# A banded attention and SOLU kernel with all its steps in a new order, w_in loaded from ScalarE, masks made on VectorE and a shorter rebuild of the sinks' values

## The chip, the cores and the metric

The kernel runs on one core of a Trainium2 chip, as one launch. The metric is the device time of the program in microseconds (us). Times of 531.01, 531.22 and 532.69 us were measured before the change; their median is 531.22 us. TensorE is called PE below, VectorE DVE, ScalarE ACT, GpSimd POOL and SyncE SP, as the profile calls them.

## The reference

Attention with a window and a few sink positions, and then a two-layer block with a normalisation between its matrix products, are computed in float32:

```python
B, H, S, D = 4, 8, 768, 64          # n_sink 4, window 128
scores = q @ k.T / sqrt(D)
keep   = (key < n_sink) | (0 <= query - key < window)
a      = softmax(where(keep, scores, -1e9))
x      = (a @ v) laid out as [B * S, H * D]          # 3072 tokens of 512
h      = x @ w_in                                    # 512 x 1024, float64 in memory
solu   = h * softmax(h)
ln     = (solu - mean) / sqrt(var + 1e-6) * g_ln
out    = ln @ w_out                                  # 1024 x 512, float64 in memory
```

The result is 3072 x 512 float32. The weights arrive as 64-bit numbers, so that the kernel has to turn their bits into float32 itself.

## The kernel before, in words

The 3072 tokens are cut into 24 chunks of 128 queries, six for each of the four batches. With a window of 128, a chunk of queries needs only its own 128 keys, the 128 before them, and the sink positions. The first chunk of a batch (chunks 0, 6, 12 and 18, "batch-first" below) has no keys before it, and so neither the second half of its scores nor the products with old values.

Float32 products are made out of pieces. Every operand is split into a high part in a type that PE multiplies fast (fp32r) and the rest, and a product is the sum of two or three such matmuls. So each chunk needs, beside its arithmetic, casts on ACT (`k_hi`, `q_hi`, `v_hi`, `x_hi`, `u_hi`, `p_hi`), subtractions for the rests on POOL (`k_lo`, `q_lo`, `v_lo`, `x_lo`) or DVE (`p_lo`, `u_lo`), and transposes on PE (`turn_q`, `turn_k`, `turn_p`, `turn_u`, `turn_sinks`), which write tiles qt, kt, ptp, utp and skp.

A chunk goes through these stages: loads of q, k and v; transposes of q and k; `score` (PE, tile s, one per head, in two PSUM buffers that the transposes of q and k share); `pick` and `mask` (DVE) which choose the half of a score tile and add the bias; `exps` (ACT); `invert` and `normalise` (DVE); transposes of the probabilities; `part_new` and `part_old` (POOL), which cut them into the new and the old half; `value` (PE, tile av); `gather` (DVE); `shift` (a copy by DMA) and `tokens` (POOL); `hidden` (PE, L611, 24 matmuls into tile h); `highest` and `peak` (DVE, L618 and L623), `solu_exp`, `solu`, `centre`, `square`, `variance` and `root`; `turn_u`; `project` (PE, L680, 24 matmuls into tile o); `scale` (ACT, L685) and `store`. The instruction of `peak`, one per chunk, is used below as the mark of a chunk's progress.

The weights come in 16 blocks of 128 x 512, eight of w_in and eight of w_out. Each block goes through `fetch_w` (a load of 512 KB from SP's queue), `size_w` (ACT, L304), `least_w`, `move_w`, `sign_w` and `rest_w` (four instructions on DVE, L311, L315, L319 and L324), for w_out `gain_w` (ACT), then `w_hi` (ACT) and `w_lo` (POOL, or DVE for four blocks). The raw words lie in buffers that later stages use too.

Two more pieces matter here. `masks` builds the biases and selectors once, from n_sink and window, which `fetch_small` loads into tile words and `scalars` turns into tile val; all of it runs on POOL (L244 to L281). `sink_values` builds, once per batch, a tile vsink out of the eight sink rows of v: on DVE seven instructions (L403, L404, L407 and L408 twice, L411).

The order of all the work is written out by hand. The table `PLAN` holds for each stage a place relative to its chunk, `PLAN_W` holds a place for each piece of weight work, and every step is sorted by `16 * n + place`, with n the chunk. Each engine then works through its own instructions in the sequence that results, and an instruction that waits holds up everything behind it on its engine. All DMAs are issued from SP's queue, in that queue's order.

## Time and profile before

| what | value |
|---|---|
| median of three runs | 531.22 us |
| the profiled execution's own time | 529.93 us |
| its span, first to last instruction | 528.2 us |
| PE busy | 466.8 us (88%), 2756 matmuls |
| DVE, ACT, POOL busy | 411.6, 373.7 and 377.1 us |
| mean granted PE clock | 0.988 |
| DMA, mean over the span | 101 GB/s |

The span is what the trace sees. The execution's own time is 1.7 us longer, and the median of the runs is another 1.3 us above that. Matmuls are pipelined, and the length shown for one (about 400 ns for 512 columns) is about twice the distance between the starts of two; so the starts are what to read. A busy share is an average over a beginning, a long middle and an end which have different limits.

### The profile page before, as it was taken

The page shows a single profiled execution, that of the slowest core. Times are in us where ns is not written, and L with a number is a line of the kernel's source. Part 1 is how long each engine was busy: PE and PEld are TensorE (multiplying, and loading weights), DVE is VectorE, ACT ScalarE, POOL GpSimd, SP SyncE. Part 2 cuts the span into 40 slices and gives each one's busy share as a digit, 9 for nine tenths or more (in the row PEclk, how much of TensorE's full clock was granted, in tenths as well). Part 3 has the DMA queues.
Part 4 walks back from the last instruction along what each step waited for, and adds up shares of the span by engine and source line. Part 5 has one row for each costly group of instructions (what it writes and reads, how often), then busy time and mean ns, then how long its engine had stood idle before and what let it go on. Part 6 is the DMA issues. An engine that isn't in the chain of part 4 may idle for free. (4 is left out here: it accounts for less than half of the span.)

```text
span 528.2 us, 9656 instructions
## 1 busy us (share of the span) xinstructions
PE 466.8 (88%) x2756; PEld 401.9 (76%) x2756; DVE 411.6 (78%) x1199; ACT 373.7 (71%) x1034; POOL 377.1 (71%) x511
## 2 busy tenths in 40 slices
PE   0054688999997999999997999999997999999995
PEld 0044567888886888888886888888886888888883
DVE  4999999987878777788688687787678778878531
ACT  3487587887785787787675688687776778766442
POOL 3969398997885387887874587778766688777520
PEclk9999998999999899999998999999999999999999
DMA  7768244333442333443532343443343344210101
GB/s 269 225 177 218 74 107 101 90 101 94 100 104 77 91 101 92 104 110 86 124 91 74 92 114 83 108 95 101 89 102 90 91 103 108 75 55 21 33 30 46
DMA packets 104203, 53.41 MB, mean 101 GB/s; under 512 B 80528, under 2 KB 92816, under 8 KB 104144
## 3 DMA queue, kind: packets, MB, share of 16 engines
q1 hardware_dynamic: 104144, 52.72, 38.6%
q8 instruction: 25, 0.41, 0.3%
q14 instruction: 34, 0.28, 0.2%
HBM read 27.53 MB, written 6.42 MB: 64 GB/s over the span
## 5 line engine op out<-in xcount | busy, mean ns | idle before, releaser
L611 PE MATMUL h<-w1h,xh 128*128 128x512 f32 x192 | 87.4, 455 | 0.0
L680 PE MATMUL o<-w2h,uh 128*128 128x512 f32 x192 | 77.9, 406 | 0.2 <-ACT uh L669 0.2
L461 PE MATMUL s<-ring,qT 128*128 128x264 f32 (+1 forms) x192 | 58.2, 312 | 22.1 <-DVE nmx L479 20.8
L611 PE MATMUL h<-w1l,xh 128*128 128x512 f32 x192 | 77.4, 403 | 0.2 <-DVE w1l L340 0.2
L611 PE MATMUL h<-w1h,xl 128*128 128x512 f32 x192 | 77.2, 402 | 0.0
L489 ACT ACTIVATE sc<-sc,nmx 128x136 f32<-128x136 f32 (+1 forms) x192 | 76.4, 405 | 0.0
L680 PE MATMUL o<-w2l,uh 128*128 128x512 f32 x192 | 75.8, 395 | 0.2 <-DVE z L641 0.2
L680 PE MATMUL o<-w2h,ul 128*128 128x512 f32 x192 | 75.8, 395 | 0.0
L578 DVE TENSOR_REDUCE y<-av 128x256 f32<-128x512 f32 x96 | 65.4, 683 | 4.9 <-PE av L572 3.4
L600 POOL TENSOR_TENSOR xl<-xt,xh 128x256 fp32r<-128x256 f32 x48 | 35.8, 745 | 39.1 <-ACT xh L596 34.2
L461 PEld LDWEIGHTS s<-ring,qT 128*128 128x128 f32 x192 | 38.6, 201 | 31.0 <-issue 19.8
L479 DVE CUSTOM_DVE_ANT_0 sc<-s,bias 128x136 f32<-128x136 f32 (+1 forms) x192 | 51.3, 292 | 13.3 <-PE s L462 10.1
L522 POOL TENSOR_SCALAR_AFFINE_SELECT pc<-pt 128x1024 fp32r<-128x1024 f32 x40 | 44.8, 1121 | 21.7 <-DVE pt L515 21.7
L462 PE MATMUL s<-ring,qX 128*128 128x264 f32 (+1 forms) x192 | 55.9, 300 | 0.1
L393 POOL TENSOR_TENSOR vs<-vn,vs 128x256 fp32r<-128x256 f32 x48 | 36.7, 765 | 20.7 <-ACT vs L388 20.7
L419 PE MATMUL qt<-ident_r,qs 128*128 128x128 f32 x192 | 23.9, 251 | 30.9 <-POOL qs L371 29.1
L500 DVE TENSOR_TENSOR sc<-sc,rs 128x544 f32<-128x544 f32 (+1 forms) x48 | 50.7, 1057 | 0.0
L591 POOL TENSOR_TENSOR xt<-y,ysh 64x256 f32<-64x256 f32 x48 | 35.9, 748 | 16.6 <-DMA ysh<-y 9.4
L528 POOL TENSOR_SCALAR_AFFINE_SELECT pt<-pt 128x1024 fp32r<-128x1024 f32 x40 | 46.6, 1166 | 1.5
L618 DVE TENSOR_REDUCE mx<-h 128x1 f32<-128x512 f32 x48 | 30.9, 686 | 21.5 <-PE h L611 21.3
L468 DVE COPY_PREDICATED s<-m_cur,s 128x128 f32<-128x128 int32 x96 | 26.5, 291 | 25.2 <-PE s L462 25.1
L419 PEld LDWEIGHTS qt<-ident_r,qs 128*128 128x128 f32 x192 | 20.9, 146 | 32.0 <-POOL qs L371 30.5
(123 smaller groups left out, 1451.2 us busy)
## 6 DMA issues: line engine op xcount, KB each, us to landing
qX<-qT SPq DMA_DIRECT2D x96, 128.0 KB, 2.3
...
```

What stands on the lines that cost most here:

```text
L393: nc.gpsimd.tensor_tensor(vs[:, :, 1:3, :], st["vn", n][:, hb * HB:(hb + 1) * HB, :].rearrange("p (r x) d -> p r x d", x=2), vs[:, :, 0:4: ...
L419: nc.tensor.transpose(tr[:, j, :], sp[:, j, :, :].rearrange("p t d -> p (t d)"), ident_r)
L461: nc.tensor.matmul(o, st["qT", n, hb][:, j, :], rhs, start=True, stop=False)
L462: nc.tensor.matmul(o, st["qX", n, hb][:, j, :], rhs, start=False, stop=True)
L479: nc.vector.tensor_tensor_reduce(out=st["sc", n, hb][:, j, c0:c1], in0=st["s", n, h].rearrange("p a x -> p (a x)")[:, c0:c1], in1=bias0 if ...
L489: nc.scalar.activation(sc[:, i, c0:c1], sc[:, i, c0:c1], AF.Exp, bias=nmx[:, i:i + 1], scale=-1.0, accum_out=ssum[:, i:i + 1])
L500: nc.vector.tensor_tensor(sc[:, :, c0:c1], sc[:, :, c0:c1], rs.unsqueeze(2).to_broadcast([P, HB, c1 - c0]), op=ALU.mult)
L522: nc.gpsimd.affine_select(pc, pt.bitcast(F32), pattern=[[0, HB * 2], [1, P]], compare_op=ALU.is_ge, fill=0.0, base=0, channel_multiplier=-1)
L528: nc.gpsimd.affine_select(pt, pt.bitcast(F32), pattern=[[0, HB * 2], [-1, P]], compare_op=ALU.is_ge, fill=0.0, base=-1, channel_multiplier=1)
L578: nc.vector.tensor_reduce(st["y", n, hb][:, jp], st["acc", n, pr].rearrange("p x s q -> p x q s"), axis=AX.X, op=ALU.add)
L611: nc.tensor.matmul(st["h", n][:, cols], a[:, kt % 2, :], w[:, kt, cols], start=(kt == 0 and m == 0), stop=(kt == KT1 - 1 and m == 2))
L680: nc.tensor.matmul(st["o", n], a[:, kt % 4, :], w[:, kt, :], start=(kt == 0 and m == 0), stop=(kt == KT2 - 1 and m == 2))
```

## The change

Five things change.

- The order: `PLAN` and `PLAN_W` get new numbers. A table `FIRST` adds an offset for the batch-first chunks. A table `OWN` gives the chunks 0, 1, 2, 3, 22 and 23 places of their own, one per step.
- The eight blocks of w_in are loaded from ACT's queue, in place of SP's, into eight buffers of their own. Those buffers are later taken by the two parts of w_out, which are now four pairs of tiles where two large ones were.
- `masks` for the biases and `barred` run on DVE, as 14 instructions, where they ran on POOL as 15; the selectors for `pick` stay on POOL.
- `sink_values` uses two instructions on ACT and three on DVE, where it used seven on DVE.
- One more small tile (`sign`) is made on POOL.

```diff
--- before.py
+++ after.py
-    "load_k": (-51.2,),
-    "load_q": (-59.1,),
...
+    "load_k": (-50.0,),
+    "load_q": (-60.35,),
...
+FIRST = {
+    "load_k": -19.1, "load_q": -20.67, "load_v": -0.71, "k_hi": -5.17, "k_lo": -2.74, "q_hi": -3.98, "q_lo": 2.77,
...
+OWN = {
+    0: (-2861.7, -2852.81, -679.14, -1022.07, -613.22, -636.58, -560.9, -1019.84, -1022.34, -648.21, -648.23,
...
+W2P = 4
...
-    wts = [consts.tile([P, r // P, m], F32R, name=nm)
-           for nm, r, m in (("w1h", DM, DFF), ("w1l", DM, DFF), ("w2h", DFF, DM), ("w2l", DFF, DM))]
+
+    wpool = ctx.enter_context(tc.tile_pool(name="wpool", bufs=2 * W2P))
+    wts = [consts.tile([P, DM // P, DFF], F32R, name=nm) for nm in ("w1h", "w1l")] + [[None] * W2P, [None] * W2P]
...
     def barred(out, keep):
-        nc.gpsimd.tensor_scalar(out, keep, 0.5, -NEG, op0=ALU.is_lt, op1=ALU.mult)
+        nc.vector.tensor_scalar(out, keep, 0.5, -NEG, op0=ALU.is_lt, op1=ALU.mult)
...
     def masks(_, j):
         if j == 0:
 
-            nc.gpsimd.tensor_scalar(near, rel, w_f, None, op0=ALU.is_lt)
-            at_least(near, near, 1)
-            nc.gpsimd.tensor_scalar(old, ki, n_f, None, op0=ALU.is_lt)
-            nc.gpsimd.tensor_copy(is_sink.rearrange("p g s -> p (g s)"), old[:, 0:NSK])
-            nc.gpsimd.tensor_tensor(old, old, near, op=ALU.add)
+            nc.vector.tensor_scalar(near, rel, 0.0, None, op0=ALU.is_ge)
+            nc.vector.scalar_tensor_tensor(near, rel, w_f, near, op0=ALU.is_lt, op1=ALU.mult)
+            nc.vector.scalar_tensor_tensor(old, ki, n_f, near, op0=ALU.is_lt, op1=ALU.max)
             barred(bias0, old)
         elif j == 1:
 
-            nc.gpsimd.tensor_scalar(old, rel, float(P), w_f, op0=ALU.add, op1=ALU.is_lt)
-            at_least(old, old, -1)
-            nc.gpsimd.tensor_tensor(old, old, near, op=ALU.add)
+            nc.vector.tensor_scalar(is_sink.rearrange("p g s -> p (g s)"), ki[:, 0:NSK], n_f, None, op0=ALU.is_lt)
+            nc.vector.tensor_scalar(old, rel, float(P), w_f, op0=ALU.add, op1=ALU.is_lt)
+            nc.vector.scalar_tensor_tensor(old, rel, 0.0, old, op0=ALU.is_lt, op1=ALU.mult)
+            nc.vector.tensor_tensor(old, old, near, op=ALU.max)
             barred(bias1[:, 4:SEG], old)
-            nc.gpsimd.tensor_scalar(far.rearrange("p g s -> p (g s)"), rel[:, 0:NSK], float(P), w_f,
+            barred(bias2[:, 4:SEG], old)
+            nc.vector.tensor_scalar(far.rearrange("p g s -> p (g s)"), rel[:, 0:NSK], float(P), w_f,
                                     op0=ALU.add, op1=ALU.is_ge)
-            nc.gpsimd.tensor_tensor(far, far, is_sink, op=ALU.mult)
-            nc.gpsimd.tensor_copy(bias2[:, 4:SEG], bias1[:, 4:SEG])
+            nc.vector.tensor_tensor(far, far, is_sink, op=ALU.mult)
...
+            nc.gpsimd.tensor_tensor(sign, even, odd, op=ALU.subtract)
...
+    def part(w, kt, cols=slice(None)):
+        return w[kt // 2][:, kt % 2, cols] if isinstance(w, list) else w[:, kt, cols]
+
     raws = {}
     three = [("u", 2), ("u", 2), ("e", 1)]
-    raw_tags = three + [("pt", 3)] * 3 + [("pc", 2)] * 2 + three * 3
 
     def fetch_w(_, j):
         _, _, src, kt, cols = blocks[j]
-        tag, bufs = raw_tags[j]
-        raws[j] = sb.tile([P, NB, 2], I32, tag=tag, name=f"wraw_{j}", bufs=bufs)
-        nc.sync.dma_start(raws[j].rearrange("p f w -> p (f w)"), src.bitcast(I32)[kt * P:(kt + 1) * P,
-                                                                                 2 * cols.start:2 * cols.stop])
+        if j < NW1:
+            raws[j] = wpool.tile([P, NB, 2], I32, tag="w2", name=f"wraw_{j}")
+        else:
+            tag, bufs = three[j % 3]
+            raws[j] = sb.tile([P, NB, 2], I32, tag=tag, name=f"wraw_{j}", bufs=bufs)
+
+        queue = nc.scalar if j < NW1 else nc.sync
+        queue.dma_start(raws[j].rearrange("p f w -> p (f w)"), src.bitcast(I32)[kt * P:(kt + 1) * P,
+                                                                               2 * cols.start:2 * cols.stop])
...
     def w_hi(_, j):
-        wh, _, _, kt, cols = blocks[j]
-        nc.scalar.copy(wh[:, kt, cols], st["w", j])
+        wh, wl, _, kt, cols = blocks[j]
+        if j >= NW1 and wh[kt // 2] is None:
+            for nm, w in (("w2h", wh), ("w2l", wl)):
+                w[kt // 2] = wpool.tile([P, 2, DM], F32R, tag="w2", name=f"{nm}_{kt // 2}")
+        nc.scalar.copy(part(wh, kt, cols), st["w", j])
...
             raw = st["vsraw", b]
-            four = sb.tile([P, 8, D], F32R, tag="ob", name=f"vsx_{b}", bufs=2)
-            hi, lo, tmp = four[:, 0, :], four[:, 1, :], four[:, 2:4, :].bitcast(F32)
-            nc.vector.tensor_copy(hi, raw)
-            nc.vector.tensor_tensor(lo, raw, hi.bitcast(F32), op=ALU.subtract)
+            four = sb.tile([P, 8, D], F32, tag="ob", name=f"vsx_{b}", bufs=2)
+            raw_odd, tmp = four[:, 0, :], four[:, 1:3, :]
+
             vk = sb.tile([P, NPAIR, 2 * D], F32R, tag="vsink", name=f"vsink_{b}", bufs=1)
-            for i, (x, y) in enumerate(((hi, lo), (lo, hi))):
-                nc.vector.tensor_scalar(tmp[:, i, :], y.bitcast(F32), odd, None, op0=ALU.mult)
-                nc.vector.scalar_tensor_tensor(tmp[:, i, :], x.bitcast(F32), even, tmp[:, i, :],
-                                               op0=ALU.mult, op1=ALU.add)
+            nc.scalar.copy(vk[:, 0, 0:D], raw)
+            nc.scalar.activation(raw_odd, raw, AF.Copy, scale=odd)
+            nc.vector.scalar_tensor_tensor(tmp[:, 0, :], vk[:, 0, 0:D].bitcast(F32), sign, raw_odd,
+                                           op0=ALU.mult, op1=ALU.add)
+            nc.vector.tensor_tensor(tmp[:, 1, :], raw, tmp[:, 0, :], op=ALU.subtract)
 
             nc.vector.tensor_tensor(vk, tmp.rearrange("p t d -> p (t d)").unsqueeze(1).to_broadcast([P, NPAIR, 2 * D]),
                                     mine.to_broadcast([P, NPAIR, 2 * D]), op=ALU.mult)
...
-    steps = [(16 * n + at, o, n, i, f) for o, f in enumerate(stages) for n in range(NCH)
-             for i, at in enumerate(PLAN[f.__name__])]
+    index = {(name, i): j for j, (name, i) in enumerate((name, i) for name in PLAN for i in range(len(PLAN[name])))}
+
+    def when(n, name, i):
+        if n in OWN:
+            return OWN[n][index[name, i]]
+        return round(16 * n + PLAN[name][i] + (FIRST.get(name, 0) if n % NC == 0 else 0), 2)
+
+    steps = [(when(n, f.__name__, i), o, n, i, f) for o, f in enumerate(stages) for n in range(NCH)
+             for i in range(len(PLAN[f.__name__]))]
```

The tables say little by themselves. What they do to the engines' rows is shown at three places. The names in the rows carry the chunk, then a running number.

The first place is DVE at the beginning of the second batch (chunk 6 is batch-first; the tiles of chunk 7 are what DVE works on there). vsx and vsink are the tiles of `sink_values`, s_7_5 the scores of chunk 7 and head 5. Before:

```order
L403 CAST vsx_1_2139<-vsraw_1_1494 128x64
L404 TENSOR_TENSOR vsx_1_2139<-vsraw_1_1494,vsx_1_2139 128x64
L407 TENSOR_SCALAR vsx_1_2139<-vsx_1_2139,odd_110 128x64
L408 SCALAR_TENSOR_TENSOR vsx_1_2139<-vsx_1_2139,even_109 128x64
L407 TENSOR_SCALAR vsx_1_2139<-vsx_1_2139,odd_110 128x64
L408 SCALAR_TENSOR_TENSOR vsx_1_2139<-vsx_1_2139,even_109 128x64
L411 TENSOR_TENSOR vsink_1_2142<-vsx_1_2139,mine_112 128x512
L468 COPY_PREDICATED s_7_5_2148<-m_cur_105,s_7_5_2148 128x128
L479 ISA sc_7_1_2164,nmx_7_1_2165<-s_7_5_2148,bias1_103 128x136
L479 ISA nmx_7_1_2165 128x1
L515 TENSOR_TENSOR pt_6_1_2155<-ptp_6_1_2111,pt_6_1_2155 128x4x128
L468 COPY_PREDICATED s_7_4_2168<-m_cur_105,s_7_4_2168 128x128
```

Now:

```order
L663 TENSOR_REDUCE y_6_0_2150<-av_6_0_2181 128x256
L553 COPY_PREDICATED s_7_7_2201<-m_cur_106,s_7_7_2201 128x128
L564 ISA sc_7_1_2098,nmx_7_1_2099<-s_7_7_2201,bias1_104 128x136
L564 ISA nmx_7_1_2099 128x1
L600 TENSOR_TENSOR pt_6_1_2165<-ptp_6_1_2107,pt_6_1_2165 128x4x128
L492 SCALAR_TENSOR_TENSOR vsx_1_2226<-vsink_1_2227,sign_112,vsx_1_2226 128x64
L494 TENSOR_TENSOR vsx_1_2226<-vsraw_1_1612,vsx_1_2226 128x64
L496 TENSOR_TENSOR vsink_1_2227<-vsx_1_2226,mine_114 128x512
L585 TENSOR_TENSOR sc_7_0_1992<-sc_7_0_1992,rs_7_0_2184 128x544
L758 TENSOR_TENSOR ul_4_0_2264<-utp_4_0_2194,uh_4_0_2254 128x512
L579 TENSOR_SCALAR rs_7_1_2266<-ssum_7_1_2100 128x4
```

The seven instructions stood between the scores of head 3 and those of heads 4 to 7; the three that are left stand behind the last score of chunk 7.

The second place is PE in a middle chunk. qt, kt, utp and ptp are transposes; h and av are matmuls. Before:

```order
L419 MATMUL qt_12_0_3379<-ident_r_91,qs_12_0_3226 128x128 x4
L461 MATMUL s_11_7_3384<-ring_115,qT_11_1_3181 128x264
L462 MATMUL s_11_7_3384<-ring_115,qX_11_1_3223 128x264
L665 MATMUL utp_8_1_3387<-ident_86,u_8_3261 128x128 x2
L611 MATMUL h_9_3287<-w1h_59,xh_9_0_3243 128x512
L611 MATMUL h_9_3287<-w1l_60,xh_9_0_3243 128x512
L611 MATMUL h_9_3287<-w1h_59,xl_9_0_3285 128x512
L665 MATMUL utp_8_1_3387<-ident_86,u_8_3261 128x128 x2
L611 MATMUL h_9_3287<-w1h_59,xh_9_1_3353 128x512
L611 MATMUL h_9_3287<-w1l_60,xh_9_1_3353 128x512
L611 MATMUL h_9_3287<-w1h_59,xl_9_1_3355 128x512
```

Now, around the same transposes of chunk 8 (utp_8_1):

```order
L504 MATMUL qt_12_1_3436<-ident_r_92,qs_12_1_3214 128x128 x4
L696 MATMUL h_9_3332<-w1h_62,xh_9_1_3371 128x512
L696 MATMUL h_9_3332<-w1l_63,xh_9_1_3371 128x512
L696 MATMUL h_9_3332<-w1h_62,xl_9_1_3399 128x512
L696 MATMUL h_9_3332<-w1h_62,xh_9_1_3371 128x512
L696 MATMUL h_9_3332<-w1l_63,xh_9_1_3371 128x512
L696 MATMUL h_9_3332<-w1h_62,xl_9_1_3399 128x512
L750 MATMUL utp_8_1_3461<-ident_87,u_8_3273 128x128 x2
L592 MATMUL ptp_11_0_3466<-ident_87,sc_11_0_3221 128x128 x4
L750 MATMUL utp_8_1_3461<-ident_87,u_8_3273 128x128 x2
L504 MATMUL kt_12_1_3473<-ident_r_92,ks_12_1_3151 128x128 x4
L652 MATMUL av_10_3_3480<-pc_10_1_3397,vs_10_1_3132 128x256
```

Transposes that stood apart between matmuls now stand together more often. Over the whole program PE goes from transposes back to matmuls 208 times before and 166 times now.

The third place is the beginning. On SP's queue, before:

```order
L299 DMA wraw_1_128<-in_moe_w_in_dram 128x1024
L299 DMA wraw_0_130<-in_moe_w_in_dram 128x1024
L299 DMA wraw_3_132<-in_moe_w_in_dram 128x1024
L299 DMA wraw_2_136<-in_moe_w_in_dram 128x1024
L200 DMA words_93<-in_n_sink_dram 128x2
L200 DMA words_93<-in_window_dram 128x2
L299 DMA wraw_5_140<-in_moe_w_in_dram 128x1024
L203 DMA sinks_v_96<-in_v_dram 32x512 x2
L299 DMA wraw_4_154<-in_moe_w_in_dram 128x1024
```

and now (w_in has gone to ACT's queue, where its blocks 1, 6 and 5 are the first three instructions):

```order
L381 DMA wraw_9_126<-in_moe_w_out_dram 128x1024
L381 DMA wraw_10_128<-in_moe_w_out_dram 128x1024
L276 DMA sinks_v_97<-in_v_dram 32x512 x2
L381 DMA wraw_8_132<-in_moe_w_out_dram 128x1024
L435 DMA kn_0_134<-in_k_dram 128x8x64
L435 DMA qn_0_136<-in_q_dram 128x8x64
L279 DMA g_sb_96<-in_moe_g_ln_dram 128x8x1
L435 DMA vn_0_178<-in_v_dram 128x8x64
L448 DMA vsraw_0_180<-sinks_v_97 128x64
L273 DMA words_94<-in_n_sink_dram 128x2
L273 DMA words_94<-in_window_dram 128x2
```

On DVE, now, from the eighth instruction on, where tile val is made of tile words:

```order
L393 TENSOR_SCALAR wbits_10_143<-wbits_10_143 128x512
L401 SCALAR_TENSOR_TENSOR wbits_1_140<-wraw_1_120,wbits_1_140 128x512
L393 TENSOR_SCALAR wbits_8_145<-wbits_8_145 128x512
L397 TENSOR_SCALAR wbits_10_143<-wbits_10_143 128x512
L397 TENSOR_SCALAR wbits_8_145<-wbits_8_145 128x512
L406 SCALAR_TENSOR_TENSOR wbits_1_140<-wraw_1_120,wbits_1_140 128x512
L406 SCALAR_TENSOR_TENSOR wbits_9_138<-wraw_9_126,wbits_9_138 128x512
L401 SCALAR_TENSOR_TENSOR wbits_8_145<-wraw_8_132,wbits_8_145 128x512
L406 SCALAR_TENSOR_TENSOR wbits_8_145<-wraw_8_132,wbits_8_145 128x512
L393 TENSOR_SCALAR wbits_5_174<-wbits_5_174 128x512
L220 TENSOR_SCALAR ok_7320<-val_58 128x1
L397 TENSOR_SCALAR wbits_5_174<-wbits_5_174 128x512
```

The loads of n_sink and window moved from the places behind four weight blocks to those behind the first loads of k, q and v; behind 15 weight instructions DVE comes to the first use of val (L220).

163 lines of the change are left out of this document (87 added, 76 removed), and 57 rows, old and new, of the table OWN.

## The prediction

> **What bounds the kernel now.** I read the page's slices of PE first, then busy times in stretches, then the rows where PE stops.
>
> ```profile
> PE   0054688999997999999997999999997999999995
> 0.00:19.00 19.00, 0.00 (x0) 0.00 (x0) 11.79 (x29) 8.36 (x13) 10.62 (x32) 1.00 0.79 283
> 19.00:82.40 63.40, 36.76 (x183) 30.58 (x184) 61.47 (x144) 42.92 (x122) 48.66 (x56) 1.00 0.56 143
> 145.20:158.40 13.20, 13.20 (x88) 11.62 (x87) 9.28 (x25) 11.27 (x36) 11.18 (x15) 1.00 0.41 103
> 514.80:528.00 13.20, 7.89 (x36) 5.43 (x34) 1.45 (x3) 4.03 (x7) 0.55 (x1) 0.92 0.13 46
> ```
>
> There are three regimes. Until about 90 us PE starves and DVE is full: from 19 to 82.4 us it works 61.47 of 63.40 us. In the middle PE is full (13.20 of 13.20) while DVE has about a quarter to spare, except at three dips, one per batch boundary. At the end PE is full up to its last matmuls. So an edit counts if it shortens DVE's work at the beginning, PE's own work in the middle, or the dips.
>
> The marks of progress, one `peak` per chunk, give the rhythm:
>
> ```profile
> 156.79 0.18 DVE L623 TENSOR_SCALAR nm<-mx 128x1 f32<-128x1 f32 x1
> 179.27 0.18 DVE L623 TENSOR_SCALAR nm<-mx 128x1 f32<-128x1 f32 x1
> 272.56 0.18 DVE L623 TENSOR_SCALAR nm<-mx 128x1 f32<-128x1 f32 x1
> 295.05 0.18 DVE L623 TENSOR_SCALAR nm<-mx 128x1 f32<-128x1 f32 x1
> 388.43 0.18 DVE L623 TENSOR_SCALAR nm<-mx 128x1 f32<-128x1 f32 x1
> 409.47 0.18 DVE L623 TENSOR_SCALAR nm<-mx 128x1 f32<-128x1 f32 x1
> ```
>
> Five ordinary chunks take 272.56 - 179.27 = 93.3 us, 18.66 each, and 388.43 - 295.05 gives 18.68. Across a boundary the step is 22.48, 22.49 and 21.04 us. A boundary thus costs 3.8, 3.8 and 2.4 us, 10.0 in all.
>
> **The boundary stalls.** What happens in the first of them:
>
> ```profile
> 164.18 0.58 DVE L403 CAST vsx<-vsraw 128x64 fp32r<-128x64 f32 x1
> 166.41 0.28 DVE L408 SCALAR_TENSOR_TENSOR vsx<-vsx,even 128x64 f32<-128x64 f32 x1
> 166.90 0.73 DVE L408 SCALAR_TENSOR_TENSOR vsx<-vsx,even 128x64 f32<-128x64 f32 x1
> 167.66 1.11 DVE L411 TENSOR_TENSOR vsink<-vsx,mine 128x512 fp32r<-128x512 f32 x1
> 168.70 0.28 DVE L468 COPY_PREDICATED s<-m_cur,s 128x128 f32<-128x128 int32 x1
> 169.47 0.36 PE L461 MATMUL s<-ring,qT 128*128 128x264 f32 x1 [2.72 <-DVE nmx L479]
> 171.00:174.00 3.00, 3.00 (x13) 2.60 (x12) 2.77 (x9) 1.66 (x4) 0.00 (x0) 0.50 0.23 55
> 402.00:404.00 2.00, 1.96 (x15) 1.60 (x14) 1.97 (x9) 1.56 (x3) 0.00 (x0) 1.00 0.01 4
> ```
>
> DVE spends 164.18 to 168.70, 4.5 us, on the seven instructions of `sink_values`. PE has filled both score buffers and waits 2.72 us for the next one. Then its granted clock is 0.50 for about 3 us, worth another 1.5 us; at the third boundary the clock stays at 1.00, and that one costs 2.4 us in place of 3.8. In the new order three DVE instructions are left. I price them at 0.28 for each small one, by the quick row, plus 1.11, so 1.7 us, or 2.6 if they meet POOL as in the slow row (0.73). They stand behind the last score of chunk 7, so no score buffer waits for them; next in line are `normalise` and `u_lo`, which PE needs only after other matmuls. PE rode out 4.5 - 2.7 = 1.8 us before, so 1.7 us should pass unseen. The two instructions moved to ACT lie between exponentials there and are as narrow; ACT worked 11.27 of 13.20 us in the full stretch above, so it can take them. I take 0.5 us per boundary as what stays: a gain of 8.5, bounds 5 and 10.
>
> **Fewer turns between transposes and matmuls.**
>
> ```profile
> 178.10 0.62 PE L507 MATMUL ptp<-ident,sc 128*128 128x128 f32 x4
> 178.48 0.48 PE L680 MATMUL o<-w2h,uh 128*128 128x512 f32 x1
> 178.80 0.40 PE L680 MATMUL o<-w2l,uh 128*128 128x512 f32 x1
> 179.04 0.39 PE L680 MATMUL o<-w2h,ul 128*128 128x512 f32 x1
> ```
>
> The first matmul behind transposes occupies 178.80 - 178.48 = 0.32 us, the next 0.24 (0.23 in long runs of them). So each return costs about 0.085 us. The order has 208 of them before and 166 now: 42 x 0.085 = 3.6 us, of which I count 3.0, since those in the starved beginning are free. Bounds 0 and 4.
>
> **The beginning.** Ahead of the first `peak` DVE had to do 11.79 + 61.47 = 73.3 us of work by 82.4 us. The rows that price what differs:
>
> ```profile
> 6.33 0.69 DVE L319 SCALAR_TENSOR_TENSOR wbits<-wraw,wbits 128x512 int32<-128x512 int32 x1
> 16.87 1.31 POOL L340 TENSOR_TENSOR w1l<-wbits,w1h 128x512 fp32r<-128x512 f32 x1
> 17.10 1.63 DVE L319 SCALAR_TENSOR_TENSOR wbits<-wraw,wbits 128x512 int32<-128x512 int32 x1
> L324 DVE SCALAR_TENSOR_TENSOR wbits<-wraw,wbits 128x512 int32<-128x512 int32 x16 | 14.9, 933 | 0.0
> L319 DVE SCALAR_TENSOR_TENSOR wbits<-wraw,wbits 128x512 int32<-128x512 int32 x16 | 13.7, 865 | 0.1
> L315 DVE TENSOR_SCALAR wbits<-wbits 128x512 int32<-128x512 int32 x16 | 9.3, 586 | 0.1
> L311 DVE TENSOR_SCALAR wbits<-wbits 128x512 f32<-128x512 f32 x16 | 8.5, 529 | 5.1 <-ACT wbits L304 5.1
> 24.23 0.87 POOL L225 TENSOR_SCALAR bias<-is_sink 128x8 f32<-128x8 f32 x1
> ```
>
> Counted in the two orders ahead of that mark, the rows are nearly the same. Now there is one more each of L311, L315 and L319 (0.53 + 0.59 + 0.87 = 2.0 us), the 14 mask instructions, and four sink instructions fewer (4.5 - 1.7 = 2.8); one `normalise` only comes later, and I leave it out. No mask instruction has a row on DVE: nine are 128 columns wide, five at most 8. A quarter of 0.69 us plus the fixed part makes about 0.22, so 9 x 0.22 + 5 x 0.15 = 2.7; the bounds are 1.5, and 14 x 0.73 = 10 if each meets POOL.
>
> Against that stands contention. The same L319 takes 0.69 us alone, 1.63 beside a POOL instruction and 0.865 in the mean, a fifth more than alone. A fifth of 15 blocks at 2.91 us is 9 us. POOL loses the masks, which filled much of its time up to 25.10 us (the row at 24.23 is the last), 10 to 13 us of the 59 that it worked by then (10.62 + 48.66): I take a quarter of the 9 us back, 2.3, bounds 0 and 6. So DVE's work is 73.3 + 2.0 + 2.7 - 2.8 - 2.3 = 72.9 us.
>
> The page of the Trainium skill "SBUF — State Buffer" (section "Who interferes with whom") speaks against masks on DVE: an instruction there with two tensor inputs and a GpSimd instruction that reads share a port, and whichever comes second is blocked until the first ends. Five of the masks have two such inputs. By the row alone they cost 0.22 each; by the rule each could wait out a POOL instruction of 1.31 us, 6.5 us more, and the sum below would be 527.6 in place of 521.1.
>
> How early does DVE get going?
>
> ```profile
> 3.39 0.47 SPq L200 DMA_DIRECT2D words<-in_window_dram  x1
> 4.72 0.66 ACT L304 ACTIVATE wbits<-wraw 128x512 f32<-128x512 f32 x1 [2.63 <-DMA wraw<-in_moe_w_in_dram]
> 9.09 0.68 ACT L304 ACTIVATE wbits<-wraw 128x512 f32<-128x512 f32 x1 [0.39 <-DMA wraw<-in_moe_w_in_dram]
> 10.96 0.19 POOL L211 CAST words_f<-words 128x4 f32<-128x4 int32 x1 [6.23 <-DMA words<-in_window_dram]
> 20.20 0.43 SPq L350 DMA_DIRECT2D qn<-in_q_dram  x1
> ```
>
> From one queue the first four blocks were there between 4.72 and 9.09 us, about 1.45 us apart, 512 KB each, near 360 GB/s, with the DMA engines 0.79 busy. Two queues side by side bring the first two blocks together at about 6.2 us, not the first at 4.7. The Trainium skill's "DMA: Bandwidth & Descriptors" (section "Issuing engines are not separate DMA queues") says that loads from several engines share the same DMA engines and save issue time only; by the idle fifth in the row the loads could land 1 to 2 us earlier by 10 us, by the rule not at all.
>
> The loads of q and k now go out at about 6 us in place of 20.20, so PE starts near 16 us, not 29; but PE is not what is short there. The words now follow them, and the request for window waits for q to land, since SP reuses the semaphores of earlier loads. Ahead of q lie six blocks of 512 KB; after the first at 4.72 us the other 3.1 MB need 8.6 us, so it goes out near 14 us. The old one took 7.6 us in the crowd (3.39 to 10.96), this one half that; val is ready near 19. DVE reaches L220 after 15 weight instructions, 10.4 us by the means, 8.3 with POOL quiet, and stands. What is late behind it is all of DVE's queue, and through it the scores. So DVE has 8.3 us done at 19 us, where it had 11.8. From there 72.9 - 8.3 = 64.6 us remain; with the old 1.9 us of gaps the first `peak` falls at 85.5, 3.1 us later. By the second `peak` PE has done 1.2 us more than it had (32.0 against 30.8 us, its rows ahead of there counted at 0.2325 us per 512 columns). Net loss 1.9; bounds a gain of 6 (no stall at L220, contention nearly gone) and a loss of 9.
>
> **The end** has one small edit.
>
> ```profile
> 515.49 1.09 PE L665 MATMUL utp<-ident,u 128*128 128x128 f32 x8
> 516.82 0.51 PE L680 MATMUL o<-w2h,uh 128*128 128x512 f32 x1 [0.24 <-ACT uh L669]
> 523.01 0.69 ACT L685 ACTIVATE ob<-o,al 128x512 f32<-128x512 f32 x1 [4.72 <-issue]
> ```
>
> Now the last three matmuls of chunk 22 stand between the last transposes and chunk 23's, and fill the 0.24 us gap and a part of the clipped start: I take 0.5 off, bounds 0 and 1. The last store still follows the scale at 523.01.
>
> **The sum.** Span 528.2 - 8.5 - 3.0 + 1.9 - 0.5 = 518.1 us. The execution's own time was 529.93, 1.7 above its span, and the median 1.3 above that: 518.1 + 3.0 = 521.1 us.
>
> **The rivals.** (1) *The beginning gains*: words land before DVE has done its 15 instructions, and contention falls by 6. Then the beginning gains 6 in place of losing 1.9: 513. For it: PE idles 46 us there (19.00, and 63.40 - 36.76). Against it: DVE's 73 us of work there are hardly fewer. (2) *The boundaries stay*: PE's idle time comes back behind another DVE instruction there, and 5 of the 8.5 us are lost: 526. For it: PE has only 1.8 us of patience there, and what now follows the sinks feeds `project`. Against it: no score waits behind them. (3) *Slower*: the new order leaves a score waiting in every ordinary chunk. The view of waits, with the total, the times and the longest:
>
> ```profile
> PE s L461 <- DVE nmx L479: 20.8, 12, 5.0
> ```
>
> PE waited for a freed score buffer 12 times, 20.8 us, nearly all in the beginning and at the boundaries. If `pick` or `mask` now stands behind an instruction that itself waits, PE loses that in each of about 20 chunks. The gains in hand are 10.1 us, so this decides from 0.5 us per chunk; at 0.8 us it costs 16 and gives 537. For it: the in-order queues and only two buffers. Against it: DVE is a quarter idle there, and the scores now stand further apart among `hidden` and `project`. (4) *The change does not do what it says*: with the same rows on the engines it would be 531; the order shows otherwise, so this has no chance of its own.
>
> **Chances.** Forecast 0.64, rival 1 0.14, rival 2 0.13, rival 3 0.09. A measurement here tells 0.3%, 1.6 us, from no change. The forecast and rival 1 are faster, rival 2 mostly: faster 0.85; no difference 0.06, from rival 2's upper part and rival 3's beginnings; slower 0.09. The forecast's own bounds, taken together, are 515 to 527. For 8 in 10 I take 512 to 528, which adds rival 1 and most of rival 2.
>
> **What would show it.** Right: no PE wait over 1 us and no clock of 0.50 at the boundaries, `peak` steps there of 18 to 19 us; ordinary steps near 18.5; the first `peak` between 82 and 88 us; an idle gap on DVE before L220. Wrong: ordinary steps above 19 us (rival 3), boundary steps still above 21 us (rival 2), or a first `peak` before 79 us (rival 1). The sum breaks if the beginning moves by more than 8 us.

## The result, and the profile after

| | before | changed | ratio, 95% interval |
|---|---|---|---|
| median of the runs | 531.18 us | 551.40 us | 1.0372 (1.0347 to 1.0397) |
| span of the profiled execution | 528.2 us | 548.7 us | |

The change costs 20 us. The forecast was 521.1 us, a gain of 10; the time lies outside its range, and the sign is wrong. Four runs gave 550.41 to 551.96 us. First the page of the changed kernel, PE's busy time and its slices, as shown of before:

```profile
PE 473.0 (86%) x2756; PEld 401.2 (73%) x2756; DVE 398.3 (73%) x1197; ACT 372.5 (68%) x1042; POOL 358.3 (65%) x497
PE   0334677999999999999998999999898999998994
```

PE works 6 us longer on the same 2756 matmuls, all other engines work less. The three dips at the batch boundaries are smaller, but the beginning is no fuller. The marks of progress (`peak`, now L708), from the timeline of the changed kernel:

```profile
88.69 0.18 DVE L708 TENSOR_SCALAR nm<-mx 128x1 f32<-128x1 f32 x1
189.44 0.21 DVE L708 TENSOR_SCALAR nm<-mx 128x1 f32<-128x1 f32 x1
286.94 0.20 DVE L708 TENSOR_SCALAR nm<-mx 128x1 f32<-128x1 f32 x1
306.37 0.21 DVE L708 TENSOR_SCALAR nm<-mx 128x1 f32<-128x1 f32 x1
529.60 0.21 DVE L708 TENSOR_SCALAR nm<-mx 128x1 f32<-128x1 f32 x1
```

The step across the second boundary is 306.37 - 286.94 = 19.4 us, where it was 22.5: the stall there is gone. Across the first boundary it is 25.4 us (164.00 to 189.44), a length that the prediction named as the sign of rival 2, but the rival's cause is not there: PE waits in that step only once for more than 0.15 us, 0.93 us for `highest`, and the two steps before it are short, 15.1 and 16.4 us. But the six chunks from 189.44 to 306.37 take 116.9 us, 19.5 each, and the ordinary step has risen from 18.7 to 19.5. The first `peak` comes 6.3 us later, the stretch from the first to the last takes 440.9 in place of 428.9 us, and what follows the last `peak` 19.1 in place of 16.9. The waits of PE, over the whole program (total, times, longest):

```profile
PE s L546 <- DVE nmx L564: 18.3, 10, 4.8
PE qt L504 <- POOL qs L456: 16.8, 2, 16.4
PE h L696 <- DVE mx L703: 12.1, 20, 1.9
```

The third row is new; before has none of its kind. PE waits 20 times, nearly once per chunk, for `highest` (L703), in the midst of `hidden` (L696).

### The profile page after: what moved, and what is told of

Read it like the earlier page. It is cut to its first block, busy times and chain, and to the rows that moved or that the text cites. A ratio compares the mean times of both kernels' runs of the same rounds, so it can differ in the third digit from the quotient of the medians.

```text
span 548.7 us, 9546 instructions
## 1 busy us (share of the span) xinstructions
PE 473.0 (86%) x2756; PEld 401.2 (73%) x2756; DVE 398.3 (73%) x1197; ACT 372.5 (68%) x1042; POOL 358.3 (65%) x497
## 5 line engine op out<-in xcount | busy, mean ns | idle before, releaser
L696 PE MATMUL h<-w1h,xh 128*128 128x512 f32 x192 | 83.9, 437 | 13.0 <-DVE mx L703 12.1
L546 PE MATMUL s<-ring,qT 128*128 128x264 f32 (+1 forms) x192 | 61.7, 323 | 20.9 <-DVE nmx L564 18.3
L696 PE MATMUL h<-w1h,xl 128*128 128x512 f32 x192 | 76.9, 400 | 0.0
L696 PE MATMUL h<-w1l,xh 128*128 128x512 f32 x192 | 76.6, 399 | 0.0
L663 DVE TENSOR_REDUCE y<-av 128x256 f32<-128x512 f32 x96 | 65.4, 684 | 11.6 <-PE av L657 4.9
L456 POOL TENSOR_TENSOR qs<-qn,qs 128x256 fp32r<-128x256 f32 x48 | 37.3, 779 | 43.7 <-ACT qs L452 42.4
L564 DVE CUSTOM_DVE_ANT_0 sc<-s,bias 128x136 f32<-128x136 f32 (+1 forms) x192 | 54.6, 294 | 14.8 <-PE s L547 9.6
L703 DVE TENSOR_REDUCE mx<-h 128x1 f32<-128x512 f32 x48 | 32.7, 684 | 30.6 <-PE h L696 30.6
L696 PEld LDWEIGHTS h<-w1h,xh 128*128 128x128 f32 x192 | 36.9, 192 | 19.4 <-DVE mx L703 16.3
L523 ACT CAST ring<-kt 128x512 fp32r<-128x512 f32 x48 | 28.2, 587 | 32.0 <-PE kt L504 31.9
L547 PEld LDWEIGHTS s<-ring,qX 128*128 128x128 f32 x192 | 39.0, 203 | 10.8 <-DMA qX<-qT 4.5
L754 ACT CAST uh<-utp 128x512 fp32r<-128x512 f32 x48 | 28.0, 585 | 26.9 <-PE utp L750 26.9
L613 POOL TENSOR_SCALAR_AFFINE_SELECT pt<-pt 128x1024 fp32r<-128x1024 f32 x40 | 44.5, 1112 | 1.0
```

The lines of the kernel that those rows point to most:

```text
L456: nc.gpsimd.tensor_tensor(sp[:, :, 1, :], st[nm + "n", n][:, hb * HB:(hb + 1) * HB, :], sp[:, :, 0, :].bitcast(F32), op=ALU.subtract)
L546: nc.tensor.matmul(o, st["qT", n, hb][:, j, :], rhs, start=True, stop=False)
L547: nc.tensor.matmul(o, st["qX", n, hb][:, j, :], rhs, start=False, stop=True)
L564: nc.vector.tensor_tensor_reduce(out=st["sc", n, hb][:, j, c0:c1], in0=st["s", n, h].rearrange("p a x -> p (a x)")[:, c0:c1], in1=bias0 if ...
L613: nc.gpsimd.affine_select(pt, pt.bitcast(F32), pattern=[[0, HB * 2], [-1, P]], compare_op=ALU.is_ge, fill=0.0, base=-1, channel_multiplier=1)
L663: nc.vector.tensor_reduce(st["y", n, hb][:, jp], st["acc", n, pr].rearrange("p x s q -> p x q s"), axis=AX.X, op=ALU.add)
```

## What that wait is

The tile h holds two halves of 512 columns, and `hidden` has eight steps of three matmuls, four for each half. In the new `PLAN` the reduction of the second half stands at 12.62, and the last two `hidden` steps, of the first half, at 12.73 and 13.02. In the old one both reductions (12.1 and 12.9) stand behind the last step (11.45). The halves do not overlap, but they are one tile: the matmul that writes into h behind a reduction that reads h carries a wait for it. It is matmul 19 of 24. In the order of PE's instructions 20 of the 24 chunks have it there, one has it at matmul 22, and before none.

One such place in the changed kernel, on PE:

```profile
256.02 0.46 PE L504 MATMUL qt<-ident_r,qs 128*128 128x128 f32 x4
256.32 0.46 PE L696 MATMUL h<-w1h,xh 128*128 128x512 f32 x1
260.82 0.45 PE L504 MATMUL qt<-ident_r,qs 128*128 128x128 f32 x4
261.86 0.50 PE L696 MATMUL h<-w1h,xh 128*128 128x512 f32 x1 [0.59 <-DVE mx L703]
```

and on DVE:

```profile
258.51 1.00 DVE L585 TENSOR_TENSOR sc<-sc,rs 128x544 f32<-128x544 f32 x1
260.25 0.69 DVE L758 TENSOR_TENSOR ul<-utp,uh 128x512 fp32r<-128x512 f32 x1 [0.73 <-ACT uh L754]
261.15 0.66 DVE L703 TENSOR_REDUCE mx<-h 128x1 f32<-128x512 f32 x1
```

The four transposes take 0.30 us (256.02 to 256.32), so the matmul was due at 261.12. It starts at 261.86, when the reduction of 261.15 has ended: 0.74 us lost, 0.59 that the view shows as idle and 0.15 that it doesn't: the end shown for a matmul lies about that far behind the start of the next one in an unbroken run. The reduction was late because DVE stood at `u_lo` (L758) for ACT just before. Twenty waits of 12.1 us in all, and 0.15 more for each, make 15.1 us.

**Theory A**: this wait makes the ordinary chunk slow. **Theory B**: the new order makes DVE late, and this wait is only where it shows. Beside these stand the terms of the prediction: boundaries, turns, beginning, end.

## Experiments on the wait

**The reduction moved ahead in the kernel before.**

```diff
-    "highest": (12.9, 12.1),
+    "highest": (12.9, 10.8),
```

> The kernel before with one number altered: the reduction of the second half of h at 10.8 in place of 12.1, so between the hidden steps 10.7 and 11.05 of the two halves. Theory A: matmul 19 of each chunk waits 0.4 to 0.8 us for the reduction, 24 chunks, ordinary steps 19.2 to 19.5, 541 to 550. Theory B: nothing is late in the old order, the reduction comes at once, steps 18.7 to 18.8, 531 to 534.

Measured: 553.91 us, ratio 1.0427 (1.0398 to 1.0456), a loss of 22 us from one number.

```profile
PE h L611 <- DVE mx L618: 19.4, 24, 1.4
```

All 24 chunks wait, 0.8 us each, and the ordinary steps rise from 18.2 to 19.2 us to 19.1 to 20.2. Theory A's mechanism stands by itself in the old order, and costs somewhat more than its upper bound.

**The reduction moved behind in the changed kernel.** `place` is the table's number.

```diff
     def when(n, name, i):
+        if name == "highest":
+            return max([place(n, name, i)] + [place(n, "hidden", j) + 0.02 for j in range(8)])
```

> The changed kernel with one thing altered: the reduction of each half of h (highest) never stands before the last hidden step of the other half. Theory A (matmul 19 of 24 into h waits for the reduction of the finished half, since both halves are one tile): 20 waits of 0.6 us and some 0.2 us each for starting again go, the ordinary step falls from 19.5 to 18.6 to 18.8 us, the wait h <- mx vanishes, and the time is 534 to 539; the first peak stays near 88.7. Theory B (PE is held up by late work of the other engines in the new order, and h <- mx is only where it shows): another wait takes its place, steps stay above 19.2, 546 to 551.

Measured: 547.14 us, ratio 1.0301 (1.0271 to 1.0331). The wait is gone, but only 4 us come back: theory B's number. The timeline shows why, on DVE

```profile
225.28 0.69 DVE L703 TENSOR_REDUCE mx<-h 128x1 f32<-128x512 f32 x1 [2.82 <-PE h L696]
225.89 0.68 DVE L758 TENSOR_TENSOR ul<-utp,uh 128x512 fp32r<-128x512 f32 x1
226.49 0.68 DVE L663 TENSOR_REDUCE y<-av 128x256 f32<-128x512 f32 x1
227.09 0.72 DVE L585 TENSOR_TENSOR sc<-sc,rs 128x544 f32<-128x544 f32 x1
227.72 0.68 DVE L703 TENSOR_REDUCE mx<-h 128x1 f32<-128x512 f32 x1
228.32 0.29 DVE L553 COPY_PREDICATED s<-m_prev,s 128x128 f32<-128x128 int32 x1
```

and then on PE:

```profile
231.42 0.36 PE L546 MATMUL s<-ring,qT 128*128 128x264 f32 x1 [0.86 <-DVE nmx L564]
```

Now DVE stands 2.82 us at the reduction until the 24th matmul has ended, with `u_lo`, `gather`, `normalise` and the picks queued behind it, and a score is late in turn. The wait had changed sides.

**Both reductions at the later of their two places**, behind those three instructions.

```diff
+        if name == "highest":
+            return max([place(n, name, 0), place(n, name, 1)] + [place(n, "hidden", j) + 0.02 for j in range(8)])
```

> The changed kernel with both reductions of h at the later of their two places, so behind the u_lo, gather and normalise that stood between them, and never ahead of the last hidden step. Theory C (in the changed kernel and in the run with the reduction right behind the last matmul, DVE itself stands at the reduction, 2.8 us at a time, and what queues behind it makes scores and outputs late): DVE's wait mx <- PE h falls from 26 us in the middle to below 8, PE's waits for nmx, y and ul go, the ordinary step falls from 19.25 to 18.6 to 18.9, and the time is 537 to 541. Theory B2 (DVE in the new order is late for reasons other than the reduction): steps stay at 19.2 or above and the time at 545 to 549.

Measured: 535.40 us, ratio 1.0085 (1.0068 to 1.0102); 16.0 us come back, more than theory C asked for. DVE's waits at the reduction in the middle (190 to 460 us): first the run before, then this one.

```profile
DVE mx L703 <- PE h L696: 26.3, 14, 3.6
```

```profile
DVE mx L703 <- PE h L696: 4.3, 5, 1.2
```

So the place of `highest` costs the changed kernel 16.0 us by the medians, close to the 15.1 counted above. With it mended the kernel is still 4.6 us slower than the one before, measured beside it. It has to stand behind the last `hidden` step, for PE, and not right behind it, for DVE. What a batch of six chunks takes is seen in windows from `peak` to `peak`: in the changed kernel, in this run, and in the kernel of the next section, which has the old order and no stall. The columns are length, busy time (and instructions) of PE, PE's weight loads, DVE, ACT and POOL, then clock, DMA share and GB/s.

```profile
208.79:325.69 116.90, 112.90 (x691) 97.07 (x690) 88.87 (x278) 86.29 (x250) 82.29 (x116) 1.00 0.41 96
```

```profile
206.72:319.53 112.81, 111.91 (x692) 96.51 (x691) 88.78 (x278) 86.27 (x250) 82.96 (x116) 1.00 0.42 99
```

```profile
191.72:302.54 110.82, 110.82 (x691) 97.24 (x690) 88.15 (x279) 87.13 (x251) 85.31 (x116) 1.00 0.42 101
```

The same work takes 110.8 us in the old order with PE never idle. In the new one, mended, it takes 112.8: 0.9 us idle in two waits (0.7 of it for qX, the swapped copy of q that a DMA makes), 0.3 that these waits cost beyond the idle time shown, and 0.8 us in which PE is busy longer.

## Experiments on the boundaries

All three edit the kernel before.

**Shorter and moved**: the body of `sink_values` and the tile `sign` from the changed kernel, and a new place.

```diff
-    "sink_values": (-12.0,),
+    "sink_values": (-6.5,),
...
-            nc.vector.tensor_copy(hi, raw)
-            nc.vector.tensor_tensor(lo, raw, hi.bitcast(F32), op=ALU.subtract)
...
+            nc.scalar.copy(vk[:, 0, 0:D], raw)
+            nc.scalar.activation(raw_odd, raw, AF.Copy, scale=odd)
...
```

> The kernel before with the shorter sink_values alone, placed at -6.5, behind the last score of the next chunk (was -12.0). Theory of the boundaries as predicted: the stall of 2.7 us and the stretch of half clock behind it go at all three, steps there 18.7 to 19.2 in place of 22.5, 22.5 and 21.0, 521 to 523.5. Rival (the stall comes back behind another instruction): 526 or more, with a PE wait above 1 us there.

Measured: 515.44 us, ratio 0.9709 (0.9678 to 0.9740): the fastest kernel of this study, 16.3 us below before.

```profile
266.49 0.18 DVE L625 TENSOR_SCALAR nm<-mx 128x1 f32<-128x1 f32 x1
284.46 0.18 DVE L625 TENSOR_SCALAR nm<-mx 128x1 f32<-128x1 f32 x1
```

The second boundary's step is 18.0 us; the same is measured at the other two. That is less than the ordinary 18.66, since a batch-first chunk has less to do: PE starts 107 matmuls in that step, 113 to 119 in the others. The stalls therefore cost 4.5, 4.5 and 3.1 us, 12.1 in all, where the prediction, counting from 18.66, saw 10.0. The span falls by 14.4 us, of which 1.0 lies ahead of the first `peak` (one rebuild of the sinks stands there). The rest of the 16.3 is that the execution profiled before was quick: the median measured beside this run, 531.74 us, stands 3.5 us above that span, the median here 1.7 above its own.

**Shorter alone, at the old place.**

> The kernel before with the shorter sink_values (two instructions on ACT, three on DVE) left at its old place, among the scores of the next chunk. If the length decides (PE rides out 1.8 us, the three take 1.7): boundary steps 18.0 to 18.6, 515 to 519. If the place decides: a PE wait of 0.5 to 1.5 us and a stretch of half clock stay at the boundaries, 520 to 526.

Measured: 519.22 us, ratio 0.9780 (0.9763 to 0.9796). Boundary steps 19.0 us; in the middle

```profile
PE s L463 <- DVE nmx L481: 1.8, 2, 0.9
```

PE still waits 0.9 us for a score buffer at each boundary. "PE rides out 1.8 us" was too kind.

**Moved alone, still seven instructions.**

> The kernel before with its seven DVE instructions of sink_values unchanged and moved to -6.5, behind the last score of the next chunk. If the place decides: no PE wait at the boundaries, steps 18.0 to 18.6, 515 to 518. If the length decides: 4.5 us of DVE there make what follows (normalise, u_lo, the next scores) late, a PE wait above 1 us stays, 521 to 529.

Measured: 523.50 us, ratio 0.9858 (0.9840 to 0.9876). Boundary steps 20.4 us; over the whole program

```profile
PE ptp L507 <- DVE sc L500: 7.3, 4, 2.9
```

One of the four lies at 64.6 us, the other three (1.4 to 1.6 us each) at the boundaries, where no score waits any more. The 4.5 us on DVE now make `normalise` late, which the prediction named as next in line, and PE waits for it at its transposes. So length and place each give a part (11.6 and 7.3 us), and only together do they clear the boundary.

## Experiments on the beginning

In the changed kernel DVE's weight work is quicker than forecast and still ends later. The groups of its four instructions:

```profile
L401 DVE SCALAR_TENSOR_TENSOR wbits<-wraw,wbits 128x512 int32<-128x512 int32 x16 | 12.3, 775 | 0.1
L406 DVE SCALAR_TENSOR_TENSOR wbits<-wraw,wbits 128x512 int32<-128x512 int32 x16 | 11.9, 763 | 0.0
L393 DVE TENSOR_SCALAR wbits<-wbits 128x512 f32<-128x512 f32 x16 | 9.0, 562 | 8.5 <-ACT wbits L386 8.5
L397 DVE TENSOR_SCALAR wbits<-wbits 128x512 int32<-128x512 int32 x16 | 7.6, 492 | 0.2
```

A block costs 2.59 us where it cost 2.91, so 16 blocks give back 5.1 us (forecast 2.3). The 14 masks take 4.3 us (forecast 2.7). DVE works 67.3 us ahead of the first `peak` (forecast 72.9), but it idles 21.4 us there, 9.1 before. Three of its stalls, the two largest among them:

```profile
6.69 0.43 DVE L393 TENSOR_SCALAR wbits<-wbits 128x512 f32<-128x512 f32 x1 [5.76 <-ACT wbits L386]
12.90 0.43 DVE L393 TENSOR_SCALAR wbits<-wbits 128x512 f32<-128x512 f32 x1 [2.27 <-ACT wbits L386]
23.15 0.15 DVE L220 TENSOR_SCALAR ok<-val 128x1 f32<-128x1 f32 x1 [5.33 <-POOL val L289]
```

The stall at val was forecast, for 19 us; it ended at 23.15.

**The words first on SP's queue.**

```diff
-    "fetch_small": (-669.55, -2920.83, -690.99),
-    "scalars": (-569.99,),
+    "fetch_small": (-4000.0, -2920.83, -690.99),
+    "scalars": (-655.0,),
```

> The changed kernel with the loads of n_sink and window first on SP's queue and their conversion ahead of the last mask step on POOL. Theory W (the beginning is late because DVE stands 5.3 us at its first use of val): val is ready before 12 us, the stall is gone, the first peak falls at 83 to 85 in place of 88.7, 546 to 548.5. Rival (the beginning is set by the order in which weight blocks land and are made, or by PE): the stall moves to another DVE wait, first peak above 87, 549.5 to 552.

Measured: 551.12 us, ratio 1.0380 (1.0348 to 1.0413). No gain, and a first `peak` at 90.6. On ACT:

```profile
12.59 1.95 ACT L386 ACTIVATE wbits<-wraw 128x512 f32<-128x512 f32 x3 [9.10 <-DMA wraw<-in_moe_w_out_dram]
```

val is ready at 10.6 us and L220 no longer waits. But the block that ACT takes first lands at 12.6 in place of 6.0 us, and DVE waits 12.4 us for it.

**The words behind three blocks**: the same edit with -2870.0.

> The changed kernel with the loads of n_sink and window on SP's queue just ahead of the first k and q and behind three blocks of w_out, and their conversion ahead of the last mask step on POOL. The first blocks keep their places, so they land as in the changed kernel (6.0 us for the first). Theory W: val is there before 16 us, DVE's stall of 5.3 us is gone, the first peak falls at 84 to 86 in place of 88.7, 546.5 to 549. Rival (k and q land later behind the words, and the late scores of chunk 0 and 1 set the first peak): first peak 87 or later, 549.5 to 552.

Measured: 548.50 us, ratio 1.0333 (1.0305 to 1.0362). The blocks land as in the changed kernel, the stall at val is gone, and yet the first `peak` is at 88.05: three waits for ACT, 1.46, 2.03 and 1.40 us, have come in its place. The time fits theory W, the first `peak` the rival. Of the 2.9 us gained 0.6 lie there.

**Parts of the change put into the kernel with the short sinks.** w_in on ACT's queue:

```diff
-        nc.sync.dma_start(raws[j]...
+        (nc.scalar if j < NW1 else nc.sync).dma_start(raws[j]...
```

> The kernel of sinks_both with w_in loaded from ScalarE's queue and nothing else. If the second queue costs: the first block lands at 6 us or later in place of 4.7, DVE's first wait grows by 1.5 to 2 us, first peak 83 to 85, 517 to 519.5. If not: 514.5 to 516.5.

Measured: 517.55 us, ratio 0.9736 (0.9706 to 0.9766). The first `peak` is 2.0 us later (83.36, was 81.39) and everything behind it as before. The first block landed at 7.2 us (4.8 in the kernel with the short sinks), and so DVE's waits for ACT's work on the blocks are longer, 7.4 us in place of 5.1:

```profile
DVE wbits L313 <- ACT wbits L306: 7.4, 2, 7.0
```

Masks on DVE, as 14 instructions at the old places:

> The kernel of sinks_both with the masks on DVE as in the changed kernel, at their old places. As predicted, 2.7 us of DVE work against 2.3 us of contention taken back: 514 to 517.5, first peak within 1.5 us of 81.4. By the rule of the Trainium skill's page SBUF — State Buffer (section Who interferes with whom), each of the five masks with two inputs waiting out a POOL instruction of 1.31 us: 520 to 522.

Measured: 519.94 us, ratio 0.9788 (0.9759 to 0.9817), first `peak` 3.7 us later. The price is not the masks' own work: they take 5.4 us, and the rest of DVE's work up to the first `peak` is 6.3 us less. It is this, on POOL

```profile
29.57 5.95 POOL L372 TENSOR_TENSOR qs<-qn,qs 128x256 fp32r<-128x256 f32 x1 [4.64 <-ACT qs L368]
36.86 0.72 POOL L372 TENSOR_TENSOR qs<-qn,qs 128x256 fp32r<-128x256 f32 x1
```

with DVE beside it

```profile
29.03 0.68 DVE L341 TENSOR_TENSOR w1l<-wbits,w1h 128x512 fp32r<-128x512 f32 x1
34.25 0.68 DVE L320 SCALAR_TENSOR_TENSOR wbits<-wraw,wbits 128x512 int32<-128x512 int32 x1
40.04 0.43 DVE L312 TENSOR_SCALAR wbits<-wbits 128x512 f32<-128x512 f32 x1 [5.10 <-ACT wbits L305]
```

The first qs takes 5.95 us, a later one 0.72. DVE has no gap from 29.03 to 34.93 us, and 0.6 us after that POOL is done. PE waits for this qs, ACT waits for PE with its next weight block behind, and DVE waits 5.1 us for ACT.

**The second group of masks moved** (-38.0 in place of -315.5) in that kernel:

> The kernel of masks_dve with the second group of masks at -38.0 in place of -315.5, so behind some 15 more weight instructions of DVE; the same work. Theory E: the meeting of the first qs with DVE's unbroken run falls out otherwise, no POOL instruction takes above 2.5 us, DVE's wait of 5.1 us near 40 us is gone, 513.5 to 516.5. Theory F: 518 to 521 as with masks_dve.

Measured: 517.41 us, ratio 0.9737 (0.9706 to 0.9760). qs takes 1.0 us, the wait of 5.1 us is gone and the first `peak` is at 82.8. The time lies between the ranges of the two theories, and another POOL instruction is held in turn, which theory E did not expect:

```profile
22.04 6.62 POOL L341 TENSOR_TENSOR w1l<-wbits,w1h 128x512 fp32r<-128x512 f32 x2 [5.75 <-ACT w1h L336]
```

Two instructions take 6.62 us here (the first 5.40 of it), 2.59 in the run before; DVE runs without a gap until 26.31. Theory E holds for the larger part: the same masks cost 4.5 us or 2 by what they make coincide. What the remaining 2 us consist of was not separated; one wait of DVE for ACT, 1.85 us at 28.16, is among them.

**The same two parts taken out of the new order** (the kernel with both reductions late), w_in back on SP, then the masks back on POOL:

> The kernel of max_late with w_in loaded from SP's queue, at the same places. In the order of before the second queue cost 2.1 us (win_act against sinks_both). If it costs the same here: 532.5 to 534.5 and a first peak 1.5 to 3 us before 87.6. If the order of the loads has been made for two queues: SP now holds the loads of k and q behind six blocks, 535 to 539.

> The kernel of max_late with the masks back on POOL. In the order of before, masks on DVE cost 4.5 us, nearly all of it through one POOL instruction (the first qs) that took 5.95 us in place of 0.73 while DVE ran without a gap. In the trace of max_late no POOL instruction is held so long. Theory E (the price is that one held instruction, not the masks): masks back on POOL gain nothing here, 534 to 538. Theory F (the masks' own 4 to 5 us of DVE work are the price): first peak 3 to 5 us earlier, 530 to 533.

Measured: 536.14 us, ratio 1.0098 (1.0074 to 1.0122), and 536.06 us, 1.0096 (1.0065 to 1.0126), against 535.40. Neither gives anything. With w_in on SP DVE's first work starts at 11.3 us,

```profile
11.34 0.43 DVE L393 TENSOR_SCALAR wbits<-wbits 128x512 f32<-128x512 f32 x1 [10.41 <-ACT wbits L386]
```

since ACT's first block is now the fourth in the queue; with the masks on POOL, DVE saves 2.4 us of work and idles 4.3 more. First `peak` 88.4 and 89.5 us, against 87.6.

**The old beginning in the new order**: no own places for chunks 0 to 3 and the old `PLAN_W`, with w_in on SP, then on ACT.

```diff
-        if n in OWN:
+        if n in OWN and n > 3:
...
-    "fetch_small": (-669.55, -2920.83, -690.99),
+    "fetch_small": (-1094.55, -912.45, -274.2),
...
```

> The kernel of max_late with the beginning as it was before: chunks 0 to 3 have no places of their own, the weight work has its places of before, and w_in comes from SP's queue. Masks on DVE, the short sinks and the new order of the other chunks stay. Theory D (the 14 us that max_late loses up to chunk 5 against sinks_both lie in the order of the beginning: which loads come first and what DVE waits for): first peak 81 to 85, chunk 5's peak at 175 to 179, 521 to 526. Rival (they lie in the masks on DVE or in the places of the ordinary chunks, which these chunks now share): first peak above 86 or chunk 5's peak above 182, 528 to 536.

> The same with w_in on ScalarE's queue as in the changed kernel; SP's queue then begins with the loads of n_sink and window. If the second queue itself costs (two queues' loads land side by side, a small load beside a large one takes as long as that, and ScalarE issues the later ones only when its compute lets it): first peak 2 to 4 us later than in the run with w_in on SP, 524 to 530. If not: within 1.5 us of it.

Measured: 543.98 us, ratio 1.0229 (1.0195 to 1.0263), and 549.57 us, 1.0346 (1.0311 to 1.0381). First `peak` 98.2 and 103.7 us: far worse, and theory D falls in this form. Both runs change the places of the first chunks and those of the weight work at once, so which of the two hurts is not shown. The held qs of 5.95 us is in both runs again, at 29.6 and 35.6 us. The two differ by 5.6 us for the second queue, more than expected.

## Why the prediction was wrong, step by step

The step that failed is what the sum puts for the ordinary chunks of the middle. It has one term there, the gain of 3.0 us from fewer turns, and puts a new wait of PE at nothing, left to rival 3. The runs showed in its place a wait for the reduction `highest` in 20 of the 24 chunks, 12.1 us idle, whose place cost 16.0 us. That is about half of the 30.3 us between forecast and time: with the reductions late the kernel still takes 535.4 us and not 521.1, and the beginning and the first chunks behind it hold most of what is left.

Where the 20.5 us between the two profiled executions lie, by the spans of the runs above:

| piece | us | from |
|---|---|---|
| shorter sinks behind the scores | -14.4 | 528.2 to 513.8 |
| place of `highest` | +12.8 | 548.7 against 535.9 |
| first `peak` | +6.2 | the run with both reductions late against the one with short sinks, here and below |
| first `peak` to that of chunk 5 | +7.6 | 99.7 against 92.1 |
| chunk 5 to chunk 21 | +8.4 | 303.3 against 294.8 |
| chunk 21 to 23 | -1.6 | 26.8 against 28.4 |
| behind the last `peak` | +1.6 | 18.6 against 17.0 |

The table takes single executions. That of the run with both reductions late was 2.2 us above the median of its runs and that of the changed kernel 1.0 below, so the place of `highest` is 12.8 us here and 16.0 by the medians. The +8.4 is about 2 us too large for the same reason: a wait of 1.94 us for qX at 381.5 us is followed there by 3.4 us at a granted clock of 0.50, and the same stretch took 301.3 and 300.8 us in the two runs that took parts out of this kernel. The +7.6 is a loss that no experiment took apart. From the first `peak` to that of chunk 5 PE is idle in waits for 4.8 us in place of 1.9, and it starts 570 matmuls in place of 552; the rest is open.

- **Boundaries** (-8.5, bounds 5 to 10). The mechanism was right: DVE's seven instructions, the two score buffers, the half clock. The size was off: 12.1 us at the three boundaries, 14.4 of the span with the rest. Its step that failed is the comparison with the ordinary 18.66 us; the right measure is a boundary without a stall, 18.0, which no row of before shows. The 1.8 us that PE was said to ride out were not there, as the short version at the old place shows. That this term's mechanism held and the forecast was still wrong is the main lesson of the case.
- **Turns** (-3.0, bounds 0 to 4). The sign was wrong. The prediction saw the first matmul behind transposes occupy 0.32 us and took the 0.085 above 0.235 for the price of a return. The changed kernel has both cases side by side, transposes ahead of transposes and ahead of a matmul:

```profile
257.08 0.60 PE L750 MATMUL utp<-ident,u 128*128 128x128 f32 x4
257.43 0.37 PE L546 MATMUL s<-ring,qT 128*128 128x264 f32 x1
257.64 0.28 PE L547 MATMUL s<-ring,qX 128*128 128x264 f32 x1
257.75 0.40 PE L696 MATMUL h<-w1h,xh 128*128 128x512 f32 x1
263.57 0.60 PE L592 MATMUL ptp<-ident,sc 128*128 128x128 f32 x4
264.00 0.38 PE L750 MATMUL utp<-ident,u 128*128 128x128 f32 x2
```

  Four transposes ahead of other transposes occupy 264.00 - 263.57 = 0.43 us, ahead of a matmul 0.35, and the matmul behind them 0.21 in place of 0.11. What the matmul seems to pay, the last transpose has saved. In this pair of places a return costs about nothing (0.02 us), and the windows above put the new order's busy time of PE 0.8 us per batch higher, not 0.75 lower.
- **Beginning** (+1.9, first `peak` +3.1). Direction right, size off: +6.3. Contention fell by more than forecast, the masks cost more, the words came 4 us later. The step that failed is "with the old 1.9 us of gaps" after the stall: DVE was not full behind it. It idles 21.4 us in all, where the working has 12.6 (85.5 - 72.9). The second step that failed is the 1.2 us of PE's work in hand by the second `peak`: the changed kernel has started 274 matmuls by then, the one before 279, and the second `peak` is 9.0 us later. (A slip without weight: 0.865 us is a quarter more than 0.69, the fifth is of the whole.) The rule on masks with two inputs, which priced them at 6.5 us, came true for one of five, 0.9 us longer than the next:

```profile
29.50 1.23 DVE L323 SCALAR_TENSOR_TENSOR scratch_f<-scratch_f,val 128x128 f32<-128x128 f32 x1
30.77 0.35 DVE L324 SCALAR_TENSOR_TENSOR scratch_f<-scratch_f,val 128x128 f32<-128x128 f32 x1
```

  In the run with masks on DVE in the old order none of the five took above 0.36 us, but two masks with one input took 1.17 and 1.30, in place of 0.22.

  What holds the new order's first `peak` near 88 us is still open. Taking out the stall at val, the second queue or the masks each made another wait of DVE grow.
- **End** (-0.5). It became +2.2 (19.1 against 16.9). The last store needs 4.7 us from issue to landing in the changed kernel, 2.6 in the one before; why was not tried.
- **Rival 3** (0.09; "decides from 0.5 us per chunk; at 0.8 us it costs 16 and gives 537"). Its price was nearly to the point: 16.0 us over 20 chunks are 0.8 us per chunk. Its place was wrong. It looked for a waiting score, because the buffers of the scores were the PSUM tiles that PE waited for in the old profile. The new wait, of PE for a reduction of h, has no row in the profile of before, and it was to be had from the tables alone: 12.62 lies between 10.08 and 12.73. "DVE is a quarter idle there" was no protection: DVE being idle on average does not make one given reduction early.

The forecast's check list worked on its own terms: ordinary steps above 19 us were named as the sign of rival 3.
